# Sigmoid attention and a gated feed-forward on one core: the products on zeros at the front, 36 of them or 19 with the same columns

## The chip, the core and the metric

The kernel runs on one core of a Trainium2 chip. The metric is the time of one execution on the device in microseconds. The kernel before takes 388.15 us (median of three runs, 387.74 to 388.28).

## The reference

```python
# q, k, v: (8 batches, 12 heads, 448 tokens, 64) float32
scores = q @ k.T / sqrt(64) - log(448)
attn   = sigmoid(scores) @ v              # no sum over the row is needed
x      = attn as (8 * 448, 768)
out    = (relu(x @ w_gate) * (x @ w_val)) @ w_out   # 768 -> 1536 -> 768, (3584, 768) float32
```

## The kernel before

One core does everything, in one program whose order is written out by hand: the Python code issues the instructions of each engine in the order in which the engine takes them, and nothing is rescheduled later. Each engine works through its own list and waits at an instruction until the semaphores it needs have the value it needs.

The work is cut by batch (8), by group of four heads (`NG` = 3) and by chunk of 64 tokens (`NCH` = 7). For each group TensorE (PE in the profile) needs keys and queries with the head dimension on the partitions. In the first batches it makes them itself: `transposed` (line 204) multiplies the fp16 rows with an identity into a PSUM tile `trt`, and VectorE (DVE) copies that to `qkT` (line 211). Later batches use DMA transposes. `qk` (line 239) makes the scores of a chunk with four 64x64 products that share the array, ScalarE (ACT) takes the sigmoid of them into `PT` (line 187), `pv` (line 257) multiplies with the values, and the feed-forward products follow (lines 322, 389, 718), with their weights as stationary operand. From about 15 us on the products of attention and feed-forward are interleaved so that TensorE always has some.

The front, up to about 14 us, is another matter, since no data are there at first. Three DMAs bring the first four heads' keys and queries in float32 (line 127), VectorE fills a tile `zeros` (128 x 448, fp16, line 130), and casts turn the arrived data into fp16 (lines 788 and 791 on VectorE, 790 and 792 on ScalarE). Batch 0 is done in slots (`FirstSlot`): six of them, a group of heads by a half of the queries (256 and 192 columns), and each slot has four units `unit(u)`, of two key chunks each (the last of one). A unit is the score products into a pair of PSUM banks (`pairp`, two such pairs) and one sigmoid of up to 128 x 1024. Between the units the dictionary `after` puts other work of TensorE, by slot and unit: transposes, values, feed-forward products.

Some of that work is on nothing but zeros: `keep_warm(count, n)` (line 172) takes a bank and issues `count` products of `zeros` with `zeros`, 128 x 128 stationary and `n` columns streamed, whose result nobody reads. They stand in these places: a burst ahead of the first transposes, while the data are on their way (line 786); a pair after them (line 798); and bursts after the units (0,1), (1,0), (1,3) and (2,0).

PSUM has eight banks. In the front four of them belong to the two pairs, and the other four form a ring (`free`): every call of `bank` takes the one at the head and puts it at the tail, so a tile waits for what was done with the bank four calls earlier. `keep_warm` makes one such call whatever its `count`. After the front the four banks of the pairs join the ring, ahead of the others.

Lines of `kernel.py` behind the change are one higher in the changed kernel.

Of the kernel before, what the change touches and what calls it, by code (L numbers as in the profile page):

```python
# [18 lines left out]
def kernel(  # L19
# [12 lines left out]
    B, H, S, D = q.shape  # L32
# [44 lines left out]
    def bank(name, shape=(P, 512), dtype=FP32):  # L77
        pool, tag = free[0]
        free.rotate(-1)
        return pool.tile(list(shape), dtype, tag=tag, name=name)  # L80
# [91 lines left out]
    def keep_warm(count, n=S):  # L172
        ps = bank("warm_ps")
        for _ in range(count):
            nc.tensor.matmul(ps[:, 0:n], zeros[:, 0:P], zeros[:, 0:n], start=True, stop=True)  # L175
# [19 lines left out]
    def pe_transposes(b, g, ti, c0=0, c1=NCH):  # L195
        transposed(b, g, ti, c0, c1)()
# [586 lines left out]


    nc.scalar.activation(gate[:], zeros[:, 0:2], AF.Sigmoid, bias=sig_bias, scale=qk_scale)
    keep_warm(22, 194)
    k16, q16, _ = in_tiles[0]
    nc.vector.tensor_copy(k16[:, 0:2, 0 : KCUT * D], first32[0])
    half = QCUT // 2 * D
# [5 lines left out]
    transposed(0, 0, 1, 0, 2)()  # L795
    transposed(0, 0, 1, 2, QCUT)()
    other_keys()
    keep_warm(2, S // 2)
    slots = [FirstSlot(half * NG + g, g, half) for half in range(2) for g in range(NG)]
    push_first(0, range(0, 2), False)  # L800
    gv_queue.append(lambda: gv_two(0, 0, 64 * HALVES[0][1], 2))
# [18 lines left out]
    def two_pv():  # L820
# [3 lines left out]

    after = {
        (0, 0): lambda: pe_transposes(0, 0, 0, KCUT, NCH),
        (0, 1): lambda: keep_warm(4, S // 2),
        (0, 2): first_of_second_group,
        (0, 3): lambda: pe_transposes(0, 1, 0, KCUT, NCH),
        (1, 0): lambda: keep_warm(4, S // 2),  # L830
        (1, 1): lambda: pe_transposes(0, 2, 0),
        (1, 2): lambda: pe_transposes(0, 2, 1, 0, QCUT),
        (1, 3): lambda: keep_warm(2),
# [233 lines left out]
```

## Time and profile before

| | |
|---|---|
| median of three runs | 388.15 us (387.74 to 388.28) |
| the profiled execution | 387.74 us, of which the span from the first to the last instruction is 386.0 us |
| mean granted TensorE clock over the span | 0.998 |
| TensorE, VectorE, ScalarE, GpSimd busy | 99%, 79%, 59%, 13% |
| products on zeros | 36 rows from 1.16 to 13.97 us: 22 of 194 columns, 10 of 224, 4 of 448 |

How to read it: the rows of the profile give the start and the length of instructions in us from the start of the span; a row that merges several gives the start of the first and the time until the last has ended. A matmul's end is modelled by the profiler, and matmuls overlap at their ends, so a product lasts longer than the distance from its start to the next one's. PE stands for TensorE's products and PEld for its weight loads. What stands in brackets is how long the engine was idle before, and what released it. "Chain" is the sequence of instructions, followed back from the last one, in which each was released by the one before.

### The profile page before, as it was taken

The numbers are of one execution on the slowest core, as the hardware profiler recorded it, in microseconds if no ns is written. First come the engines' busy times: TensorE is split into PE (matmuls) and PEld (weight loads), VectorE is DVE, ScalarE is ACT, GpSimd is POOL, SyncE is SP. The second block draws the span as 40 slices with busy tenths as digits, with TensorE's granted clock in tenths as the row PEclk, the third lists the DMA queues.
The fourth block names the chain that finished last, engine by engine and source line by source line (L and its number), as shares of the span: only waits on it lengthen the run. The fifth ranks groups of instructions, "written<-read, shape, count | busy, mean of one in ns | idle before, by whom it ended". The sixth has DMA issues, their size and how long they took to land.

```text
span 386.0 us, 8983 instructions
## 1 busy us (share of the span) xinstructions
PE 380.7 (99%) x3570; PEld 223.2 (58%) x3570; DVE 305.1 (79%) x611; ACT 227.1 (59%) x480; POOL 51.2 (13%) x76
## 2 busy tenths in 40 slices
PE   8999999999999999999999999999999999999996
PEld 6678776885555545455555554545455555555564
DVE  3455667769868999999868789999978788999663
ACT  5967887567777645455777764545477344333322
POOL 8643307000400003000301400000000000000000
PEclk9999999999999999999999999999999999999999
DMA  9999999999979302962499995222012220000236
GB/s 176 198 200 204 204 194 164 208 208 128 182 167 177 83 2 35 163 116 48 37 194 222 186 223 92 47 51 50 0 36 71 72 73 0 2 0 0 75 91 166
DMA packets 67595, 43.81 MB, mean 114 GB/s; under 512 B 35680, under 2 KB 64224, under 8 KB 67552
## 3 DMA queue, kind: packets, MB, share of 16 engines
q0 software_dynamic: 28992, 23.24, 40.5%
q1 hardware_dynamic: 37792, 19.34, 24.7%
q10 hardware_dynamic: 768, 0.66, 0.5%
q8 instruction: 28, 0.46, 0.5%
q14 instruction: 15, 0.12, 0.1%
HBM read 47.19 MB, written 11.01 MB: 151 GB/s over the span
## 4 chain that ended last, share of the span: by engine, by line
PE 97%; ACT 2%; DVE 0%; issue 0%
PE u L389 35%; PE g L389 16%; PE y L389 12%; PE qk_ps L239 10%; PE pv_ps L257 8%; PE g_ps L322 5%; PE v_ps L322 5%; PE u L718 2%; PE g L718 2%; ACT PT L187 2%; PE trt L204 1%; PE warm_ps L175 1%; DVE qkT L211 0%; DVE ysb L544 0%; DVE zeros L130 0%
## 5 line engine op out<-in xcount | busy, mean ns | idle before, releaser
L187 ACT ACTIVATE PT<-qk_ps 128x448 f16<-128x448 f32 (+3 forms) x318 | 150.9, 586 | 78.7 <-PE qk_ps L239 78.6
L389 PEld LDWEIGHTS <-S 128*128 128x128 f16 x576 | 56.4, 98 | 45.9
L628 DVE TENSOR_TENSOR gsb<-g,gsb 128x448 f32<-128x448 f32 x72 | 42.7, 624 | 7.8 <-PE g L389 7.5
L239 PE MATMUL qk_ps<-qkT 64*64 64x448 f16 (+2 forms) x756 | 47.3, 336 | 0.6 <-ACT PT L187 0.3
L389 PEld LDWEIGHTS <-hT 128*128 128x128 f16 x318 | 29.5, 98 | 24.0 <-issue 6.1
L257 PE MATMUL pv_ps<-PT,v 64*64 64x448 f16 (+2 forms) x756 | 36.6, 329 | 0.0
L468 DVE SCALAR_TENSOR_TENSOR ysb<-y,ysb 128x384 f32<-128x384 f32 x33 | 18.3, 556 | 20.6 <-PE y L389 14.1
L184 DVE TENSOR_SCALAR xT<-pv_ps 128x448 f16<-128x448 f32 (+2 forms) x53 | 27.8, 566 | 7.4 <-PE pv_ps L257 6.2
L389 PEld LDWEIGHTS <-wg 128*128 128x128 f16 x216 | 20.2, 98 | 21.8 <-issue 4.3
L389 PEld LDWEIGHTS <-wv 128*128 128x128 f16 x216 | 21.1, 98 | 19.7
L450 ACT ACTIVATE ysb<-u 128x384 f32<-128x384 f32 x28 | 13.7, 490 | 30.9 <-PE u L389 26.8
L389 PE MATMUL u<-wo,hT 128*128 128x384 f16 x156 | 29.8, 327 | 0.0
L239 PEld LDWEIGHTS <-qkT 64*64 64x64 f16 x756 | 17.7, 105 | 20.6 <-issue 14.3
L257 PEld LDWEIGHTS <-v 64*64 64x64 f16 x756 | 21.4, 107 | 11.1 <-issue 0.7
L111 POOL DMA_DIRECT2D k<-in_k_dram x15 | 11.5, 768 | 119.9 <-DVE rel L222 114.3
L389 PE MATMUL u<-xT,wg 128*128 128x448 f16 x108 | 23.5, 354 | 0.0
L389 PE MATMUL u<-X,S 128*128 128x448 f16 x108 | 23.4, 352 | 0.0
L389 PE MATMUL g<-xT,wg 128*128 128x448 f16 x108 | 23.4, 352 | 0.0
L389 PE MATMUL u<-X,wv 128*128 128x448 f16 x108 | 23.4, 352 | 0.0
L389 PE MATMUL g<-X,S 128*128 128x448 f16 x108 | 23.4, 352 | 0.0
L389 PE MATMUL g<-xT,S 128*128 128x448 f16 x108 | 23.4, 352 | 0.0
L389 PE MATMUL u<-xT,wv 128*128 128x448 f16 x108 | 23.4, 352 | 0.0
(98 smaller groups left out, 564.6 us busy)
## 6 DMA issues: line engine op xcount, KB each, us to landing
out_dram<-ysb SPq DMA_DIRECT2D x53, 192.0 KB, 3.1
v<-in_v_dram POOLq DMA_DIRECT2D x8, 336.0 KB, 12.5
v<-in_v_dram POOLq DMA_DIRECT2D x16, 168.0 KB, 13.2
wo<-in_moe_w_out_dram POOLq DMA_DIRECT2D x2, 1152.0 KB, 19.0
k<-in_k_dram POOLq DMA_DIRECT2D x10, 224.0 KB, 11.8
k<-in_k_dram POOLq DMA_DIRECT2D x3, 672.0 KB, 10.0
q<-in_q_dram POOLq DMA_DIRECT2D x3, 672.0 KB, 14.8
q<-in_q_dram POOLq DMA_DIRECT2D x8, 224.0 KB, 12.2
```

The costliest lines, as they stand in the source:

```text
L111: nc.gpsimd.dma_start(t16[:, xs, cs], rows_of(src, b)[:, xs, cs])
L175: nc.tensor.matmul(ps[:, 0:n], zeros[:, 0:P], zeros[:, 0:n], start=True, stop=True)
L184: nc.vector.tensor_scalar(out=xT, in0=src, scalar1=XSCALE, scalar2=None, op0=AOP.mult)
L187: nc.scalar.activation(PT_ap, ps_ap, AF.Sigmoid, bias=sig_bias, scale=qk_scale)
L239: nc.tensor.matmul(out_of(hh)[o : o + 64, :], qkT[rows, c, cols], qkT[rows, NCH + c0 : NCH + c1, cols], start=True, stop=True, tile_positi ...
L257: nc.tensor.matmul(ps[hh][64 * r : 64 * r + 64, 0:qn], v16[rows, 2 * g + hh, c * D : (c + 1) * D], pieces[c][rows, hh, :], start=(c == 0), ...
L322: nc.tensor.matmul(ps[:, 0:qn], (wg, wv)[i][:, dc, f * P : (f + 1) * P], xT_tiles[b][:, dc, q0 : q0 + qn], start=(dc == 0), stop=(dc == ND ...
L389: nc.tensor.matmul(ps[:, 0:n], A[:, k_, :], W[:, k_, :], start=(first and k_ == 0), stop=(k_ == kn - 1), skip_group_check=True,)
L450: nc.scalar.activation(o, ps[:, 0:HM], AF.Copy, scale=OUT_SCALE)
L468: nc.vector.scalar_tensor_tensor(out=o, in0=ps[:, 0:HM], scalar=OUT_SCALE, in1=o, op0=AOP.mult, op1=AOP.add)
L628: nc.vector.tensor_tensor(out=gs[u][i][:], in0=ps[u][:, 0:S], in1=gs[u][i][:], op=AOP.add)
L718: nc.tensor.matmul(ps[j // 2][:, j % 2 * SQ : (j % 2 + 1) * SQ], sets[j][i][:, k_, :], W[:, k_, :], start=(first and j % 2 == 0 and k_ == ...
```

## The change

The products on zeros in four of their places are replaced by fewer with more columns. The number of streamed columns stays the same in each place: 22 x 194 = 9 x 448 + 236 = 4268, 2 x 224 = 448, and 4 x 224 = 2 x 448 (twice). `keep_warm` without its second argument takes `S` = 448 columns. That makes 17 products fewer, each with the weight load before it: over all six places 36 products become 19. The first burst now consists of two calls, so it takes two banks of the ring instead of one. The bursts after the units (1,3) and (2,0) stay as they are.

```diff
@@ -783,7 +783,8 @@
     nc.scalar.activation(gate[:], zeros[:, 0:2], AF.Sigmoid, bias=sig_bias, scale=qk_scale)
-    keep_warm(22, 194)
+    keep_warm(9)
+    keep_warm(1, 236)
     k16, q16, _ = in_tiles[0]
...
@@ -795,7 +796,7 @@
     other_keys()
-    keep_warm(2, S // 2)
+    keep_warm(1)
     slots = [FirstSlot(half * NG + g, g, half) for half in range(2) for g in range(NG)]
...
@@ -824,10 +825,10 @@
     after = {
         (0, 0): lambda: pe_transposes(0, 0, 0, KCUT, NCH),
-        (0, 1): lambda: keep_warm(4, S // 2),
+        (0, 1): lambda: keep_warm(2),
         (0, 2): first_of_second_group,
         (0, 3): lambda: pe_transposes(0, 1, 0, KCUT, NCH),
-        (1, 0): lambda: keep_warm(4, S // 2),
+        (1, 0): lambda: keep_warm(2),
         (1, 1): lambda: pe_transposes(0, 2, 0),
```

## The prediction

> **What bounds the kernel now.** I read the page first (busy time and the chain that ended last), then the chain in order of time for the front, then the timeline of the front engine by engine, and last narrow cuts of that timeline around the products on zeros.
>
> ```profile
> PE 380.7 (99%) x3570; PEld 223.2 (58%) x3570; DVE 305.1 (79%) x611; ACT 227.1 (59%) x480; POOL 51.2 (13%) x76
> ...
> PE 97%; ACT 2%; DVE 0%; issue 0%
> ```
>
> TensorE is busy for 380.7 of 386.0 us and carries 97% of the chain, so whatever shifts the moment at which TensorE becomes the bound shifts the end by as much. The change touches only the first 11 us, where that is not yet so:
>
> ```profile
> 1.16 3.74 PE warm_ps L175 x22
> 4.90 0.87 PE trt L204 x12
> ...
> 5.79 0.52 DVE qkT L211 x2
> ...
> 6.34 0.44 PE qk_ps L239 x8
> ...
> 6.80 3.34 ACT PT L187 x4
> ...
> 10.17 2.87 ACT PT L187 x3
> ...
> 13.08 0.41 PE qk_ps L239 x8
> 13.49 0.48 PE warm_ps L175 x2
> ```
>
> These are pieces of the chain: start, length, what. The products on zeros (warm_ps) lead up to the first transposes, VectorE's copies lead to the first scores, and from 6.80 to 13.04 the sigmoids on ScalarE are the chain. Only the first 22 products and the last pair (which stays as it is) stand in it; the eight of 224 columns between 7.32 and 10.61 do not. For the first 22 the chain is misleading, as the timeline of the front shows:
>
> ```profile
> 4.41 0.43 DVE L788 CAST k<-ysb 128x512 f16<-128x512 f32 x1 [3.31 <-DMA ysb<-in_k_dram]
> ...
> 4.89 0.40 PEld L204 LDWEIGHTS <-k 128*64 128x64 f16 x8 [0.38 <-DVE k L788]
> ...
> 5.89 0.36 PE L175 MATMUL warm_ps<-zeros 128*128 128x224 f16 x2
> ...
> 6.34 0.41 PE L239 MATMUL qk_ps<-qkT 64*64 64x256 f16 x8
> ...
> 7.32 0.56 PE L175 MATMUL warm_ps<-zeros 128*128 128x224 f16 x4
> ...
> 10.05 0.56 PE L175 MATMUL warm_ps<-zeros 128*128 128x224 f16 x4
> ...
> 13.42 0.55 PE L175 MATMUL warm_ps<-zeros 128*128 128x448 f16 x2
> ```
>
> The first transpose's weight load stood idle for 0.38 us and was released by VectorE's cast of k (4.41 + 0.43 = 4.84), which had waited for the DMA. The data opens the transposes, at the very moment at which the products run out (4.90). Products that end earlier would gain nothing; products that end later would delay everything. The same fence shows the two forms side by side: four of 224 columns take 0.56, two of 448 take 0.55.
>
> **The change part by part.** The instruction streams of the two kernels, set side by side, differ on TensorE alone: 17 products and 17 weight loads fewer, and one wait more. Every other engine and queue has the same instructions in the same order.
>
> *The 22 of 194 columns become nine of 448 and one of 236 (4268 columns in both).* Narrow cuts of the timeline give the starts of the first and last product as 1.16 and 4.53: 21 spacings in 3.37 us, 0.160 each, or 0.827 ns a column. If the pace goes by columns, 448 take 0.371 and 236 take 0.195. The tenth product then starts at 1.16 + 9 x 0.371 = 4.50 and ends at 4.50 + 0.195 + 0.21 = 4.90, where 0.21 is what a 194-column product lasts beyond its spacing (0.37 less 0.16). The 22nd of before ends at 4.53 + 0.37 = 4.90. Difference 0.00. Were there a fixed share in each spacing, the burst could only end sooner, and the cast would still set 4.89. Bounds: 0 for a gain, because of that wait; for a loss, one granule of rounding, +0.03. I take 0.
>
> *Two of 224 become one of 448 (line 798).* After the release of the clock, starts in the row of 7.32 are 7.32, 7.43, 7.52 and 7.62: 0.11, then 0.10 for 224 columns; the rows of 448 start at 13.42 and 13.62: 0.20. So two of 224 take 0.21 and one of 448 takes 0.20. The next product, the scores at 6.34, waits for VectorE's last copy (5.79 + 0.52 = 6.31 in the chain). A gain of 0.01 falls into that wait. The cover is about 0.09, the idle time before 6.34; a loss would show only beyond it.
>
> *Twice, four of 224 become two of 448 (after the score units (0,1) and (1,0)).* From the first such product to the following scores: 10.05 to 10.54, 0.49; with two of 448, 13.42 to 13.90, 0.48. So 0.01 each, and both lie beside sigmoids: ScalarE runs without a gap in the stretch 6.80 to 10.15 and again from 10.17 to 13.04. At 7.88 the scores wait for a PSUM pair that the first sigmoid (6.80 to 7.82) still reads, so nothing moves there. At 10.54 they end at 10.95 and the next sigmoid can't start before 11.09, so there the cover is 0.14. Gone this cover, the two would be worth -0.02.
>
> *Weight loads.* 17 loads fewer; the cut rows have them at 0.15 each, beside the product before (spacing 0.16), so they add nothing now and 0 is saved.
>
> *The bank and the added wait.* The first burst is now two calls of keep_warm and so takes two banks of the four-bank ring. All later tiles move one bank on, which renames the banks and leaves every distance in the ring as it was. What is left is one wait: the first transpose of q now waits until the ninth product on zeros is done, since it writes that product's bank. Queued behind it on TensorE are the other transposes and the first scores; VectorE's copy at 5.79 waits for it. By the spacing above the ninth product is done at 1.16 + 8 x 0.371 + 0.371 + 0.21 = 4.71, and the transposes of q start at 5.33: 0.6 us of cover, cost 0. Bounds: 0 to the 0.05 that separates the cast's end (4.84) from the weight load that it releases (4.89), if checking a wait cost as much again; I take 0, since the same kind of wait stands four transposes later in both kernels, and that row (5.33, eight in 0.64, as the eight before) shows no dent.
>
> **The clock.** That is the one resource that the products exist for. Eight transposes take 0.64 at 4.90 and again at 5.33, but 0.41 at 8.22; products of 194 columns space at 0.16, and of 224 at 0.10. The granted clock's row has no lower figure in the front, so these lengths are the evidence: TensorE runs at half pace until about 5.9 us, that is 4.7 us after its first product, and at full pace from then on. By columns the change keeps the occupation of every stretch, so I take the release as unmoved.
>
> The Trainium skill ("TensorE: Matmul & The Clock Gate", Part 1) says that release goes by activity in a free-running window of about 3.4 us, a budget of time and not a number of matmuls. By that rule the count of products does not matter, and the sum stays 0. The same section says that the moment differs between runs with the window's phase. No run here shows this yet: one trace has one release.
>
> **Sum.** 0.00 + 0.00 (0.01 hidden) + 0.00 (0.02 hidden) + 0.00 = 0.00 against the profiled execution, whose time is 387.74 (span 386.0 and 1.7 around it). That execution is the fastest of the three; the others took 388.15 and 388.28. I put the forecast at the median, 388.15, rounded to 388.2; what a measurement of this kernel can tell from no change is about 0.2%, 0.8 us.
>
> **Rivals.** *No difference (my forecast), 387.4 to 388.9.* For it: the arithmetic above, and that every changed product but the first burst lies beside ScalarE.
>
> *The clock is granted later, slower.* The release may answer to the number of products or weight loads (22 loads of 0.15 in the first burst fill 3.4 us, ten fill 1.5) and not to columns. Place: the release at 5.9. Decides: whether the first stretch still counts as busy enough. Price: the nearest row for another try is the 4.7 us of the first, so a release at 10.6. By then, delayed, TensorE would have done what now stands between 5.9 and 9.2: six products on zeros at 0.10 (0.6), three and a half groups of scores at twice 0.10 (0.7) and 28 transposes at 0.25 for eight (0.9), 2.2 us at full pace and as much again at half. Slack on TensorE there: 0.33 before 9.71, 0.09 before 6.34, 0.08 before 7.88, in all 0.5. So up to 1.7 later; about 1.3 if the sigmoids absorb part. Take 1.5: 389.7. If the grant came only with the dense products at 14.83, the same count gives 14 products on zeros (1.8), ten groups of scores (2.0) and 56 transposes (1.75), 5.6 more, less about 1 of slack: 392.7. Against: half pace itself goes exactly by columns, so the array seems equally occupied. By that section of the Trainium skill, time and not number decides, and this rival would fall away.
>
> *The clock is granted sooner, faster.* Longer unbroken products might count as busier. Had it been full at 4.90, the sixteen transposes would take 0.87 less half, and VectorE's copies, four of about 0.28, would become the bound. Gain at most 0.4, 387.75: within 0.2%. To pass 0.8 it would need a cause outside this sum, such as before having been granted late in the runs that were not traced; nothing in the trace speaks for it.
>
> *The change does not do what it says.* The bank's rotation or the added wait could cost something: up to 0.05, 388.2, not to be told from none.
>
> **How the numbers follow.** No difference 0.60 (with it the last rival and most of the sooner grant); slower by the clock 0.27, of which most lies at 389.0 to 389.9 and a little near 392.7; faster by over 0.2% 0.13, for a release in untraced runs that this trace can't show. The time is that of the first, 388.2. Its own range is 387.4 to 388.9. The range that holds it 8 times in 10 goes up to the likely price of the late clock, 389.7, and down to 387.3; the upper tail and a large gain are left out.
>
> **What would show it.** In the changed kernel's timeline: one row of nine products of 448 from 1.16 with starts 0.37 apart; the weight load of k at 4.89, still released by the cast; eight transposes in 0.64 at 4.90 and 5.33; one product of 448 at 5.89 lasting 0.35; scores at 6.34, the first sigmoid at 6.80, the eighth ending near 13.5. The forecast is wrong if the product at 5.89 or the two at 7.32 still space at 0.37, if transposes after 6.6 keep 0.64 for eight, if ScalarE has gaps between 6.80 and 13.04, or if the first scores leave 6.34 by more than 0.1.

## The result and the profile after

The changed kernel takes 388.57 us (median of 22 executions, 387.82 to 390.03), the kernel before 387.93 us beside it (22, 387.45 to 388.79): ratio 1.002, 95% interval 1.0014 to 1.0025. That is +0.64 us, or 0.2%, at the very edge of what the prediction called no difference, and real: the interval excludes 1. The forecast was 388.2, and 387.4 to 388.9 for its case.

Where the time is can be seen before any row is read: every execution has its own span. The spans of the changed kernel have a median of 386.6 us, those of before 386.0 (76 executions that ran beside the experiments). The time outside the span is 1.85 against 1.81. So 0.6 us is lost between the first and the last instruction. The profiled execution of the changed kernel is not typical of that: 388.71 us with a span of 386.0 and 2.71 outside.

The front came out as the sum had it. The chain in order of time, after (start, length, what):

```profile
6.26 0.44 PE qk_ps L239 x8
...
6.72 3.35 ACT PT L187 x4
...
10.09 2.87 ACT PT L187 x3
```

And the timeline of the front, after, the rows that answer to those of before:

```profile
1.16 3.74 PE L175 MATMUL warm_ps<-zeros 128*128 128x448 f16 x10 [1.16 <-DVE zeros L130]
4.32 0.43 DVE L789 CAST k<-ysb 128x512 f16<-128x512 f32 x1 [3.21 <-DMA ysb<-in_k_dram]
4.83 0.40 PEld L204 LDWEIGHTS <-k 128*64 128x64 f16 x8 [0.55 <-DVE k L789]
...
5.80 0.36 PE L175 MATMUL warm_ps<-zeros 128*128 128x448 f16 x1
```

Ten products end where 22 ended (1.16 + 3.74 = 4.90 in both). The transposes are again opened by the cast, which in this execution came 0.09 earlier because its DMA did. Scores start at 6.26 instead of 6.34, the first sigmoid at 6.72 instead of 6.80. Nothing is lost up to here: this trace is 0.08 us ahead of that of before.

It falls behind much later, in work that the change does not touch. First TensorE's products and weight loads near 27 us, before:

```profile
26.82 0.58 PE L204 MATMUL trt<-ident,q 128*64 128x128 f16 x14
27.23 0.56 PE L204 MATMUL trt<-ident,k 128*64 128x128 f16 x14
27.72 0.28 PE L239 MATMUL qk_ps<-qkT 64*64 64x192 f16 x4
```

and the same stretch after:

```profile
26.74 0.58 PE L204 MATMUL trt<-ident,q 128*64 128x128 f16 x14
27.15 0.77 PE L204 MATMUL trt<-ident,k 128*64 128x128 f16 x14
27.85 0.28 PE L239 MATMUL qk_ps<-qkT 64*64 64x192 f16 x4
...
27.10 0.34 PEld L204 LDWEIGHTS <-k 128*64 128x64 f16 x10
27.61 0.14 PEld L204 LDWEIGHTS <-k 128*64 128x64 f16 x4 [0.18 <-issue]
```

Ahead by 0.08 at 26.74, behind by 0.13 at 27.85: the fourteen transposes of k take 0.77 instead of 0.56, because the weight loads stop for 0.18 with "issue" as the releaser. The trace shows no semaphore, no data and no engine that was waited for. That TensorE had no instruction is a reading, and the theory P below. Of these 0.21 us some come back: from 30 us to the end this trace stands 0.06 behind that of before, so its stop cost 0.14 net.

### The profile page after: what moved, and what is told of

Read it like the earlier page. It is cut to its first block, busy times and chain, and to the rows that moved or that the text cites. A ratio compares the mean times of both kernels' runs of the same rounds, so it can differ in the third digit from the quotient of the medians.

```text
span 386.0 us, 8949 instructions
## 1 busy us (share of the span) xinstructions
PE 380.6 (99%) x3553; PEld 221.0 (57%) x3553; DVE 304.8 (79%) x611; ACT 227.3 (59%) x480; POOL 51.0 (13%) x76
## 4 chain that ended last, share of the span: by engine, by line
PE 96%; ACT 2%; DVE 0%; issue 0%; ACTq 0%
PE u L389 35%; PE g L389 16%; PE y L389 12%; PE qk_ps L239 10%; PE pv_ps L257 8%; PE g_ps L322 5%; PE v_ps L322 5%; PE u L718 2%; ACT PT L187 2%; PE g L718 2%; PE warm_ps L175 1%; PE trt L204 1%; DVE qkT L211 0%; DVE ysb L544 0%; DVE zeros L130 0%
## 5 line engine op out<-in xcount | busy, mean ns | idle before, releaser
L468 DVE SCALAR_TENSOR_TENSOR ysb<-y,ysb 128x384 f32<-128x384 f32 x33 | 18.4, 556 | 20.7 <-PE y L389 14.1
```

Of the source, the lines that this page charges most:

```text
L468: nc.vector.scalar_tensor_tensor(out=o, in0=ps[:, 0:HM], scalar=OUT_SCALE, in1=o, op0=AOP.mult, op1=AOP.add)
```

## The theories

*P, pages.* The trace records an instruction queue, whose size fits TensorE's program:

```profile
q8 instruction: 28, 0.46, 0.5%
```

This is the line of before's page (packets, MB, share of 16 DMA engines); after's, which counts up to the last instruction, has 27; its 28th came later. 0.46 MB in 28 packets is 16 KB each; with 7140 instructions of TensorE in before (3570 products, 3570 weight loads) that is 255 to 256 instructions a packet, here called a page. The stop in after stands at TensorE's 959th and 960th instruction (the 480th product with its weight load). By the trace, the third transfer, which is taken to bring the page that begins there, ran from 25.38 to 26.32 in after, and from 24.67 to 25.62 in before. So the theory is: a change of 34 instructions at the front shifts every later instruction against the page edges. The stretch between two edges (instructions 704 to 960) took 21.82 to 27.07 in before, 5.25 us; in after the same number of instructions took 22.65 to 27.4, 4.8 us. If the next page needs about 5 us from the entry into the last one, before just has that and after has not.

The Trainium skill ("Runtime: NRT & Kernel Launch", Instruction fetch mechanics) states blocks of 16 KiB, 256 instructions, fetched by the engine's sequencer, with the cost of crossing an edge "mostly hidden". The size agrees with the 28 packets here; the 0.18 above was not hidden.

*C, clock.* Fewer, longer products change when the clock is granted, or make that less certain: the prediction's rival.

*L, longer products.* The longer products in the later places hold up the score products behind them, and with them the sigmoids.

P can be tried alone: empty instructions (NoOps) on TensorE right behind the first burst move the edges and change no product and no streamed column. Under P they give the time back where they restore the count of before and take time where they spoil it; under C and L they do nothing.

## The experiments

In each, `before` ran beside the experiment on the same chip. "Instructions" is against the kernel before.

**The first burst alone** (24 instructions fewer).

```diff
-    keep_warm(22, 194)
+    keep_warm(9)
+    keep_warm(1, 236)
```

> Only the first burst is changed (nine of 448 and one of 236); the later bursts are as before. 24 TensorE instructions fewer than before. Theory P (instruction pages): TensorE's instructions come in pages of 256 (28 packets of 16 KB in the instruction queue for 7140 instructions), a page is asked for when the one ahead of it is entered, and can be used about 5.0 us later; 256 instructions that run faster than that stall. In before the page from 21.82 to 27.07 takes 5.25, in the changed kernel the page from 22.65 would take 4.8 and there is a hole of 0.18 at 27.4 that no wait explains. With 24 fewer the page still takes 5.23: no hole, ratio to before 1.000 (0.9995 to 1.0008). Theory C (clock): fewer products in the first burst move the grant of the full clock: most of the loss is here, 1.0015 to 1.002. Theory L (longer products in the later bursts hold up the sigmoids): 1.000.

Measured: 388.73 (387.74 to 390.44, 9 executions) against 387.86; ratio 1.0028 (1.0013 to 1.0042). As great a loss as the whole change, which P, by its length of the page, had not expected. Part of it is outside the span: 2.13 there at the median, more than 2.1 in five of nine and up to 3.36, against 1.81 and never over 1.94 in 76 executions of before. Its trace has no stop at 27; it waits for data instead (0.2 us near 14.9 for `v`, 0.3 us near 19.6 for `wv` in `v_ps`, line 322) and for VectorE at 211 us (0.6 us, line 468). By the products' starts, set against those of before, the three cost 0.43, 0.47 and 0.73 us. So this execution's loss has other parts than a stop.

**The three later places alone** (10 instructions fewer).

```diff
-    keep_warm(2, S // 2)
+    keep_warm(1)
...
-        (0, 1): lambda: keep_warm(4, S // 2),
+        (0, 1): lambda: keep_warm(2),
...
-        (1, 0): lambda: keep_warm(4, S // 2),
+        (1, 0): lambda: keep_warm(2),
```

> Only the three later bursts are changed (2 x 224 to 1 x 448, twice 4 x 224 to 2 x 448); the first burst is 22 x 194 as before. 10 TensorE instructions fewer than before. Theory P: the page takes 5.27, no hole, ratio 1.000 (0.9995 to 1.0005). Theory C: the first burst is intact, 1.000 to 1.0005. Theory L: all of the loss, 1.0015 to 1.002.

Measured: 388.29 (387.61 to 389.82, 12) against 387.86; ratio 1.0014 (1.0004 to 1.0024). P's size for this one (none) was a miss as well, but the kind of loss is P's. The row of fourteen transposes that begins at 26.98 breaks in two:

```profile
27.98 0.25 PE L204 MATMUL trt<-ident,q 128*64 128x128 f16 x2 [0.47 <-issue]
```

The page arrived here from 25.55 to 26.53, almost a microsecond later than in before, and TensorE resumed 1.45 later. From entering the page before, at 22.07, that is 5.9 us: the "about 5 us" of the theory is no constant.

**The whole change with 34 empty instructions** (as many instructions as before).

```diff
     keep_warm(9)
     keep_warm(1, 236)
+    for _ in range(34):
+        nc.tensor.nop(hint="pad", nofuse=True)
```

> The changed kernel with 34 empty instructions on TensorE's list behind the first burst, which do nothing on the array. Theory P: the pages begin where they began in before, no hole at 27.4, ratio to before 1.000 (0.9995 to 1.0008). Theories C and L: products and columns are those of the changed kernel, so 1.0015 to 1.0025.

Measured: 387.93 (387.81 to 388.85, 11) against 387.86; ratio 1.0009 (1.0001 to 1.0018). The ratio lies between the two forecasts, nearer to that of P, and its interval overlaps that of the change (1.0014 to 1.0025); the executions themselves say more. Nine of the eleven lie at or below 388.00; of the changed kernel's 34 timed executions (with the repeat below) three do. The median of the spans is 386.1 instead of 386.6. Products and columns are those of the changed kernel, so by the medians most of the loss is not in them. One line speaks against a simple count of stops: the traced execution of this kernel has one too, of 0.21, where its own 960th instruction is:

```profile
27.25 0.41 PE L204 MATMUL trt<-ident,q 128*64 128x128 f16 x7 [0.21 <-issue]
```

By the starts of the products, this stop cost 0.38 us net against before, more than the 0.14 in the first trace of the changed kernel. So one trace doesn't show how the padding saves time, and a stop at this edge is not all of it.

**The kernel before with 40 empty instructions** (products and columns of before).

```diff
     keep_warm(22, 194)
+    for _ in range(40):
+        nc.tensor.nop(hint="pad", nofuse=True)
```

> The kernel before with 40 empty instructions on TensorE's list behind the first burst. All products as in before. Theory P: the pages begin 40 instructions earlier in the work; the page from 15.3 to 20.1 then takes 4.83, so a hole of about 0.15 appears near 20.1 in the profiled execution and more in others: ratio 1.001 to 1.003. Theories C and L: nothing about the products is changed, 1.000 (0.9995 to 1.0005).

Measured: 388.47 (388.28 to 389.01, 11) against 387.86; ratio 1.0019 (1.001 to 1.0028): the loss of the change, without the change. The place was half a miss. A step of 0.18 stands at 20.7, at instruction 704 as P has it (the same product is at 20.0 in before); the greater part comes earlier, when TensorE's products for `v_ps` wait for a weight tile (19.10 in before):

```profile
19.68 0.83 PE L322 MATMUL v_ps<-xT,wv 128*128 128x256 f16 x6 [0.50 <-DMA wv<-in_moe_w_val_dram]
```

`wv` landed at 19.63 instead of 18.73. The delay begins at GpSimd, which issues these loads in order and stood 2.10 instead of 0.44 for a piece of `v` (GpSimd's issue of k in this kernel, then in before):

```profile
13.80 0.70 POOL L111 DMA_DIRECT2D k<-in_k_dram  x1 [2.10 <-DMA v<-in_v_dram]
```

```profile
12.02 0.70 POOL L111 DMA_DIRECT2D k<-in_k_dram  x1 [0.44 <-DMA v<-in_v_dram]
```

An instruction page moves among these very loads (11.42 to 12.31 by the trace), but so it does in before (11.63 to 12.53). That it delays `v` is argued, not shown.

**The changed kernel again, with another profile.** No edit.

> The changed kernel once more, for a second profiled execution: that of the first has a span of 386.0, where most of its executions have 386.6. Theory P (instruction pages): a hole in front of the 960th TensorE instruction (about 27.4 us), without a wait that explains it, larger than the 0.18 of the first trace, or a later landing of the first weights (wv at 18.9 there). Theory C (clock): full clock later than 5.9 us, or lost again. Ratio 1.0015 to 1.0025 either way.

Measured: 388.35 (387.43 to 390.24, 12) against 387.82; ratio 1.0014 (1.0001 to 1.0028). Its trace has the stop at the same instruction, 0.22 us:

```profile
27.43 0.30 PE L204 MATMUL trt<-ident,k 128*64 128x128 f16 x4 [0.22 <-issue]
```

The front was 0.46 us ahead of before, with the clock granted at 4.55 instead of 5.87; behind the stop only 0.12 of that was left.

**The kernel before with 16 empty instructions** (the edit above with 16).

> The kernel before with 16 empty instructions behind the first burst. Theory P: the two tightest pages last 5.6 us each instead of 6.0 and 5.24, so no hole at all: ratio 0.9985 to 1.0000, and less spread. Theory C: products are those of before, 1.000. A third theory, that empty instructions as such cost time on TensorE's list (those 40 did), gives about 1.0008.

Measured: 387.92 (387.53 to 388.76, 12) against 387.82; ratio 0.9998 (0.9989 to 1.0007). No stop but a step of 0.13 at 26.9, again at instruction 960. Neither a gain nor a loss: 16 empty instructions cost nothing as such.

**The kernel before with 88 empty instructions** (the edit above with 88), which puts instruction 704 into the scores.

> The kernel before with 88 empty instructions behind the first burst. Theory P: the page from 14.6 to 18.2 would last only 3.6 us, some 1.3 less than a page needs to come: a hole of 1 to 1.4 us near 18.2, ratio 1.002 to 1.0035. Theory C: 1.000. If empty instructions as such cost time, the cost grows with the number: 40 cost 0.6 us, 88 would cost 1.3, but at the front, ahead of the transposes at 4.9, and not as a hole at 18.2.

Measured: 394.19 (392.82 to 394.4, 4) against 387.82; ratio 1.0151 (1.0133 to 1.017). TensorE's products:

```profile
8.20 0.64 PE L204 MATMUL trt<-ident,k 128*64 128x128 f16 x8 [3.41 <-issue]
...
24.76 0.35 PE L239 MATMUL qk_ps<-qkT 64*64 64x192 f16 x5 [1.41 <-issue]
```

The second line is what was to be seen: a stop of 1.41 at the 308th product (88 + 2 x 308 = 704), of the size expected and at the instruction that the count gives; its time is 24.8 because the kernel was already 4.9 us late there (the scores that before starts at 10.54 start at 15.46), and 6.5 us behind the stop. The 4.9 had not been expected. So many empty instructions were no longer hidden behind the wait for k: the transposes start at 8.20. In that idle time the clock was lost. Windows of the same trace (length, busy time and instructions of each engine, then the granted clock, DMA share and GB/s):

```profile
5.00:8.20 3.20, 0.00 (x1) 0.03 (x1) 0.00 (x0) 0.29 (x1) 3.20 (x6) 0.96 1.27 176
8.20:12.00 3.80, 3.80 (x44) 2.06 (x44) 1.35 (x5) 1.61 (x2) 3.23 (x5) 0.50 1.29 191
```

So of the 6.5 us only the 1.6 at the stop bear on pages; the total of this run is no measure of them.

**The first burst alone with 24 empty instructions** (the count of before).

> The first burst changed as in first_only, with 24 empty instructions behind it, so that all later TensorE instructions have the place in their page that they have in before. Theory P: the loss of first_only (1.0028) is gone, 1.000 (0.9995 to 1.0008). Theory C: the burst is that of the changed kernel, so 1.0015 to 1.003.

Measured: 387.77 (387.42 to 389.92, 11) against 387.82; ratio 1.0005 (0.9992 to 1.0018). At the median the loss of 0.87 is gone. The time outside the span is back at 1.82 (at most 1.89, against up to 3.36), and the span at 385.9. The row that broke in two in after is whole:

```profile
26.91 0.56 PE L204 MATMUL trt<-ident,k 128*64 128x128 f16 x14
```

**The later places alone with 10 empty instructions** (the count of before).

> The later bursts changed as in later_only, with 10 empty instructions behind the first burst, so that all later TensorE instructions have the place in their page that they have in before. Theory P (instruction pages): the loss of later_only (1.0014) is gone, 1.000 (0.9995 to 1.0008). Theory L (longer products in the later bursts): 1.001 to 1.0015.

Measured: 387.92 (387.44 to 388.71, 11) against 387.72; ratio 1.0005 (0.9996 to 1.0014). No stop. The ratio is in the range of P and below that of L, though its interval reaches into it. It is the third pair in which the padding lowers the loss, here from 0.43 to 0.20, which these numbers alone could not prove.

**Three more profiles: the changed kernel twice, the first burst alone once.** No edits, one execution each.

> The changed kernel for a third profiled execution, which may fall into its usual span of 386.5 to 386.9 (the first two had 386.0 and 385.8). Theory P: the hole ahead of the 960th TensorE instruction (480th product) is there again, 0.2 to 0.7, or TensorE waits for wv near 19. Theory C (clock): full clock granted after 7 us or lost again, with no hole.

> The same for a fourth: as for the third. If both have a hole at the 480th product, all four traces have it and the kernel before has none there.

> The kernel with only the first burst changed, for a second profiled execution: the first showed waits for the DMAs of v (14.9) and wv (19.6) and no hole at the page's end. Theory P as stated: no hole, since the page lasts 5.2 us; if a hole shows at the 480th product, a page needs more than 5.2 us here. If wv lands near 19.6 again, its late landing belongs to this kernel; near 18.7, it was one execution's.

Measured: 387.94 (span 386.0), 388.55 (span 386.4) and 388.01 (span 386.2) beside 387.72 for before. The fourth trace of the changed kernel shows the stop again, larger:

```profile
27.94 0.30 PE L204 MATMUL trt<-ident,k 128*64 128x128 f16 x4 [0.35 <-issue]
```

The third does not; there TensorE had already waited 0.39 for `wv` at 19.24, and the page, on its way from 25.15 to 26.10, was in time. In the fourth, TensorE had also waited for a later piece of `wv` near 23, which cost it 0.32. The repeat of the first burst has neither a stop nor, with 1.81, any time lost outside; `wv` landed at 18.97, so the landing at 19.59 belonged to one execution and not to this kernel.

Over all traces: the transfer of the page that begins at instruction 960 starts at 24.35 to 24.77 in before and the four kernels that hold its count or 16 more, and at 24.90 to 25.55 in the seven traces of kernels with fewer instructions. Of those seven, four stop (weight loads idle for 0.18 to 0.63, products for up to 0.47); of the five, one (0.37 and 0.21). Where TensorE stopped, it went on 1.3 to 1.6 us after the transfer had ended. In before the page ended at 25.62 and was needed at 27.05, 1.43 later: that kernel stands just on the good side.

## Why the prediction was right, and what it had not counted

The number was right in part by luck: the sum came to 0, and a real loss of 0.64 us, from a cause that is not in it, just fits into a range of 0.2% to each side.

*Each stretch of products takes the time of its columns: held.* The starts in the first burst of after are 0.35 and then 0.373 to 0.374 apart (0.371 in the working), the tenth starts at 4.495 (4.50), the burst ends at 4.90 (4.90).

*The cast opens the transposes: held,* with 0.55 of idle time before the weight load instead of 0.38.

*The 0.01 for each later place, hidden: held.* From the products at 9.97 to the following scores it is 0.48 to 0.49, ScalarE runs through from 6.72 to 12.96, and no row shows a gain or loss.

*The rotated bank and the added wait at zero: held.* The transposes of q start at 5.25, with no idle time, and the first scores 0.46 after the product at 5.80 (0.45 in before).

*The clock is unmoved: held in the main, and better founded now.* The trace's clock record grants full speed at 5.71 in after, at 5.87 in before. But these two are no measure. Over all traces it is granted between 4.18 and 7.12 with the longer products in the first burst (both ends in the kernel with that burst alone), and between 4.54 and 6.75 with the first burst of before. The stretches at full clock measure whole multiples of 3.413 us (378.88 is 111 of them, 382.29 is 112), so the grant falls on the edge of a window that runs free of the kernel. That is what the Trainium skill ("TensorE: Matmul & The Clock Gate", Part 1) states of the window. Where the grant falls moves the front and stays to the end: the grant at 4.55 put it 0.46 ahead of before, where the prediction had at most 0.4, and that at 7.12 put it 0.28 behind. With 4.54 to 4.79 in the three further traces of the changed kernel the first scores stand at 5.88 to 5.94, more than 0.1 from 6.34. That is one of the prediction's own signs of being wrong, but it was read off one trace, with one moment of the grant. Six of the eight traces with the longer products in the first burst have the grant at 5.33 or sooner, and one of the six with that of before; so few can't tell chance from a shift, and a sooner grant would work against the loss. The rival "granted later" is not the cause of the median loss: with the same products, empty instructions took most of it away.

*17 weight loads fewer at zero: this step was mis-sized.* It counted the time of the removed instructions on the engine, beside the products, and rightly found none. It did not count that 34 instructions fewer move the rest of the program against its pages. Measured, the number of instructions alone is worth +0.6 us in one direction (before with 40 empty ones) and takes the median of the change's loss from 0.64 to 0.07 in the other; the ratios, which count the long executions too, go from 1.002 to 1.0009. By medians, in us against before beside it on the same chip:

| instructions against before | products of before | products of the change, whole or part |
|---|---|---|
| 0 | 0 | +0.07 (whole), -0.05 (first burst), +0.20 (later places) |
| +16 | +0.10 | |
| +40 | +0.61 | |
| -10 | | +0.43 (later places) |
| -24 | | +0.87 (first burst) |
| -34 | | +0.64 and +0.53 (whole) |

Shown is that the time hangs on the count. The kernel before with 40 empty instructions is slower with its products untouched. No pair of padded and unpadded kernels proves as much alone, since their intervals overlap, but all three go the same way, and together the spans have a median of 386.5 in the 58 executions with fewer instructions, 386.1 in the 33 padded back, and 386.0 in the 76 of before. The bank's rotation and the added wait are in the padded first burst too, so they are not the cause. Shown is also that TensorE stops at instructions 704 and 960 where the count puts them, in traces, with products idle for up to 1.41 us. How the stops add up to the medians is not shown: three traced executions of the changed kernel lost 0.14, 0.35 and 0.47 net at the stop and the padded one lost 0.38, and in the traces with other counts part of the loss is a late `wv` instead (waits of 0.31, 0.39 and 0.50 us: the first burst alone, the third trace of the whole change, before with 40). A second part may lie at the end. The last page is fetched at 379.4 in before, inside the span, but at 387.3 to 389.4 in the changed kernel and the one with the first burst alone (their traces that show it), behind the last instruction; and only kernels with fewer instructions have executions with more than 2.1 us outside the span. That the late page makes them is not shown: the third trace of the changed kernel and the repeat of the first burst have it too, with 1.94 and 1.81 outside.

Open are three things. The kernels with 24 and 10 instructions fewer lose, although their page up to instruction 960 is as long as in before (5.2 to 5.3 us): the transfer started 2.3 to 3.9 us after the page before it was entered, over all traces, and what sets that was not found. Why `v` and `wv` land later in some alignments, and in some executions of one, was not tried. And six of 91 executions of kernels with longer products had spans of 387.7 or more, against none of 99 with the products of before (the 88 left out); a clock granted a window late, a rare form of the rival, may be behind them. The mean granted clock (0.996 to 1.000) doesn't tell: in before's trace it is lowered only after the last product (382.44), from 384.74 on. None of them was traced, and at some 1.6 us each they would be 0.1 us of a mean.

No version ran faster than the kernel before by more than the intervals allow.

## What to carry to other kernels

An edit that removes instructions from an engine that is never idle has two prices: the time of the instructions, and where it puts all later ones against the pages in which the program is fetched. When a change of no cost on paper moves the time by 0.1 to 0.3%, as here, pad it with empty instructions to the old count before looking for a cause in the change itself, and compare many executions: one trace of a padded kernel can have the stop too. Look at the spans first, then for idle time released by "issue" far behind the edit.

## What the runs showed of the hardware

TensorE's program comes in pages of 16 KB (28 packets of that size), and the stops stand at instructions 704 and 960, 256 apart. Over all fourteen traces the transfer for instruction 960 started 2.3 to 3.9 us after instruction 704 was entered and took 0.9 to 1.0 us. Where TensorE stopped, it went on 1.3 to 1.6 us after the transfer's end, which was 5.0 to 5.9 us after it had entered the page before. These stops, with "issue" as the only sign, left the weight loads idle for 0.18 to 0.63 us near 27 us, and the products for 1.41 us at 24.8 in the kernel with 88 empty instructions.

Empty instructions on TensorE were free while it waited for data (16 cost nothing, and 40 left the transposes at 4.83), but not without limit: 88 of them held it until 8.20 us, so each took at most (8.20 - 1.16) / 88 = 0.08 us.

An idle time of 3.41 us cost the clock for two windows: the record of that trace shows half speed from 7.95 to 14.78, 6.8 us. So 88 instructions that do nothing cost 6.4 us at the median. In the traced execution, 6.6 us longer, about 3.3 of them are the late start, 1.6 were lost by 15.46, mostly at half speed, and 1.6 at the stop at instruction 704.
